# Sparse attention and a gated FFN on one core: the first K third through the casting queue, small tables over two issuers, and filler matmuls in column tiles

## The chip, the cores and the metric

The kernel runs on one core of a Trainium2 chip. Its engines are TensorE (PE, with its weight loads PEld), VectorE (DVE), ScalarE (ACT), GpSimd (POOL) and SyncE (SP). SP and ACT issue plain DMAs; POOL issues DMAs that change the type from float32 to float16 on the way. The metric is device microseconds (us) of one execution.

## The reference

```
q, k, v: 4 x 8 x 768 x 64 (batch, head, token, dim), float32
mask[i, j] over blocks of 32 tokens: |block i - block j| <= 1, or one of the two
    is the first or the last block, or j's block is one of 3 sampled for i's block
a = softmax(q k^T / 8 where mask else -1e9) v
x = a as 3072 tokens x 512
out = (sigmoid(x w_gate) * (x w_val)) w_out        # 512 -> 1536 -> 512
```

The output is 3072 x 512 in float32. The sampled blocks are an input, so the mask is made on the chip.

## The kernel before

The 3072 tokens are cut into twelve query chunks of 256 (three for each batch entry), and the eight heads into four pairs. For one chunk and pair (`attend`) there are three score tiles of two blocks of 128 keys each. A tile is made on PE by matmuls of 64 rows that stand in pairs in the two halves of the array, one for each head (L617); ACT takes the exponential (L635) and writes `pt`; DVE multiplies with the 0/1 mask (L643). When three tiles are done, 24 value matmuls follow (L658), DVE normalises (L666, L669), and the result is transposed into `xT`: on PE for the first three chunks (L694, copied by DVE at L699), by a DMA transpose later. In the first chunk the mask is not multiplied: extra matmuls (`e24` with `bias`, also L617) add a large negative number to masked scores, so that the exponential makes zeros of them.

The FFN (`ffn`) works on one query chunk of 256 tokens: for each of twelve blocks of 128 hidden units four gate and four value matmuls (L720), a tanh on ACT (L739), a product on DVE (L746); then twelve output matmuls for each of two blocks of 128 tokens (L764), scaled by 0.5 on ACT or DVE and stored by SP.

The order of the instructions on each engine is made by a planner (`Plan.run`), when the kernel is built. Each operation gets an engine, a duration, a priority and what it needs; the planner steps through a time of its own and gives each engine the best operation that is ready by that time. A load may name the time at which it is taken to have landed (`lands`, with the constants `LAND_K`, `LAND_Q`, `E24`). On the chip each engine then runs its list in order and waits where something is late. Where PE has nothing to do before the planned time `SPIN`, the planner puts in filler matmuls on a zero tile (`spin_op`, L364). From the `CHAIN`-th pair of chunk and head pair on, the order on PE is written out as fixed rounds (`ROUND`): score tiles, value matmuls, FFN and output matmuls. `FETCH` says behind which score tile the loads of the next batch entry may be issued; those of the second entry wait for the load of the second third of `wo` too.

The head of the kernel matters here. Of the first head pair of batch entry 0, K comes whole by SP into `k_in` (float32, L467) and a third of Q, the token positions that the first chunk needs (`early`, two of six), into `q_in` (L471). ACT casts the same third of K (`k_a`, L474) and of Q (`q_a`, L475), DVE casts the rest of K (`k_b`, L476). All the other loads of batch entry 0, in the order of `FIRST`, go by POOL with a cast (`load_half`, L423), and behind them the weights `wg`, `wv` (L503) and `wo` (L512), each in two or three parts. Q and K are then transposed on PE (`turn_pe`, L441) against the identity `ident16` and copied out of PSUM by ACT or DVE (L449, L447).

The small tables are `ident16`, `sbi` (the sampled blocks) and `mi` (fixed part of the mask and an index row), issued in this order by ACT (L342 to L344), and `e24` (which token is in which block), which SP loads twice, into rows 0 to 23 and 64 to 87 (L348). From `mi` and `sbi`, four small DVE operations (`blocks`, L540 to L546) make the mask of blocks, `mb16`. One matmul with `e24` (`expand`, L557) widens it, and DVE makes `bias` of it (L564). The array is used in three shapes: whole ("full"), in half rows ("row": scores and mask) and in half columns ("col": transposes of Q and K).

Of the kernel before, what the change touches and what calls it, by code (L numbers as in the profile page):

```python
# [9 lines left out]
f16 = mybir.dt.float16  # L10
f32 = mybir.dt.float32
# [6 lines left out]
NB = S // BLK  # L18
NJ = S // 128
# [8 lines left out]
VW = 66  # L28
SPIN = 22.0
NMASK = 1  # L30
FETCH = ((7, 1), (1, 2))
CHAIN, GLAG, OLAG, ROUND = 16, 5, 9, "SoVgggoo"
EDGES = [0, 768, 1536]
LAND_K, LAND_Q, E24 = 4.0, 4.7, 4.2
FIRST = [
    ("k", 1), ("q", 1), ("k", 2), ("q", 2), ("v", 0), ("q", 0), ("k", 3), ("q", 3), ("v", 1), ("v", 2), ("v", 3),
]
# [223 lines left out]
def kernel(  # L261
# [11 lines left out]
    nc = tc.nc  # L273
# [4 lines left out]
    e24_h = nc.inline_tensor(e24_np, name="bb_e24")  # L278
# [3 lines left out]
    mi_h = nc.inline_tensor(mi_np, name="bb_mdet_iota")  # L282
    id_h = nc.inline_tensor(np.eye(128, dtype=np.float16), name="bb_ident")
# [5 lines left out]
    src = {  # L289
        nm: [a[b].rearrange("h (p j) d -> p h j d", j=NJ) for b in range(B)]  # L290
        for nm, a in (("q", q), ("k", k), ("v", v))
    }
    outv = out.rearrange("(b p j) m -> b j p m", p=128, j=NJ)

    P = Plan()
# [11 lines left out]
    def sb(tag, shape, dt):  # L307
        n = len(P.rings[tag])
        return Buf(tag, lambda i: work.tile(shape, dt, tag=tag, bufs=n, name=tag))
# [4 lines left out]
    def psb(shape, dt=f32, homes=SINGLE, span=1):  # L314
        def make(i):
            t = psum[:, i : i + span].rearrange("p b c -> p (b c)")
            if dt != f32:
                t = t.bitcast(dt)
            n = int(np.prod(shape))
            t = t[:, 0:n]  # L320
            if len(shape) == 2:
                t = t.rearrange("p (a b) -> p a b", a=shape[0])
            return t

        b = Buf("ps", make)
        b.homes, b.span = homes, span
        return b

    def one(shape, dt, name):
        b = Buf(None, None)  # L330
        b.tile = sing.tile(shape, dt, name=name)
        return b


    ident16 = one([128, 128], f16, "ident16")
    sbi = one([NB, 3], mybir.dt.int64, "sbi")
    mi = one([NB, 2 * NB], f32, "mi")
    e24 = one([128, NJ, 128], f16, "e24")
    zero = one([128, 128], f16, "zero")
    P.op("DVE", 0.1, lambda: nc.vector.memset(zero(), 0.0), writes=[zero], prio=-91)  # L340
    P.op("DVE", 0.3, lambda: nc.vector.memset(e24(), 0.0), writes=[e24], prio=-99)
    P.op("ACT", 0.4, lambda: nc.scalar.dma_start(ident16(), id_h.ap()), writes=[ident16], prio=-99, dma=0.1, lands=3.0)  # L342
    P.op("ACT", 0.6, lambda: nc.scalar.dma_start(sbi(), sampled_blocks), writes=[sbi], prio=-98, dma=0.1, lands=3.4)  # L343
    P.op("ACT", 0.4, lambda: nc.scalar.dma_start(mi(), mi_h.ap()), writes=[mi], prio=-97, dma=0.1, lands=3.8)  # L344
    for i, r in enumerate((0, 64)):
        P.op(
            "SP", 0.45,
            lambda r=r: nc.sync.dma_start(e24()[r : r + NB].rearrange("b j q -> b (j q)"), e24_h.ap()),  # L348
            writes=[e24], prio=(-96, -93)[i], dma=0.2, lands=E24,
        ).deps[1:] = []  # L350
    vring = [one([128, 2, NJ, VW], f16, f"v16_{i}") for i in range(8)]
    for i in range(8):
# [3 lines left out]
            writes=[vring[i]], prio=-80 + i,  # L356
        )

    def spin_op(dur, fresh):
        if fresh:  # L360
            P.spun = psb([128])
        t = P.spun
        return P.op(
            "PE", dur, lambda: nc.tensor.matmul(t(), zero(), zero(), start=True, stop=True),  # L364
            reads=[zero], writes=[t], prio=1e6, mode="full",
        )

    P.spin, P.spin_op, P.spin_until = zero, spin_op, SPIN


    every, early, later = slice(0, NJ), slice(0, 2), slice(2, NJ)
# [42 lines left out]
    def load_half(nm, b, p, prio, dur=0.72):  # L414
        cut = (nm, b, p) == ("q", 0, 0)
        js = later if cut else every
        if cut:
            c = one([128, 2, NJ - 2, 64], f16, "q16_late")
        else:
            c = sb(f"{nm}16" if nm != "v" else "vh", [128, 2, NJ, 64], f16)  # L420
        half16[nm, b, p] = stage[nm, b, p] = c
        o = P.op(
            "POOL", dur, lambda: nc.gpsimd.dma_start(c(), src[nm][b][:, 2 * p : 2 * p + 2, js]),  # L423
            writes=[c], prio=prio, dma=0.8 if cut else 1.0,
        )
        o.slack = 0.3 + b
        return o
# [24 lines left out]
    def turn_dma(nm, b, p, prio):  # L452
# [6 lines left out]
            reads=[c], writes=[t], prio=prio, dma=1.3,  # L459
        )  # L460

    k_in = one([128, 2, NJ, 64], f32, "k_in")
    q_in = one([128, 2, 2, 64], f32, "q_in")
    k_a, k_b = one([128, 2, 2, 64], f16, "k16_a"), one([128, 2, NJ - 2, 64], f16, "k16_b")
    q_a = one([128, 2, 2, 64], f16, "q16_a")
    P.op(
        "SP", 0.5, lambda: nc.sync.dma_start(k_in(), src["k"][0][:, 0:2]), writes=[k_in], prio=-95, dma=1.0,  # L467
        lands=LAND_K,
    )
    P.op(  # L470
        "SP", 0.5, lambda: nc.sync.dma_start(q_in(), src["q"][0][:, 0:2, early]), writes=[q_in], prio=-94, dma=0.7,  # L471
        lands=LAND_Q,
    )
    P.op("ACT", 0.35, lambda: nc.scalar.copy(k_a(), k_in()[:, :, early]), reads=[k_in], writes=[k_a], prio=-88)  # L474
    P.op("ACT", 0.35, lambda: nc.scalar.copy(q_a(), q_in()), reads=[q_in], writes=[q_a], prio=-88)  # L475
    P.op("DVE", 0.42, lambda: nc.vector.tensor_copy(k_b(), k_in()[:, :, later]), reads=[k_in], writes=[k_b], prio=-67)  # L476
    for i, (nm, p) in enumerate(FIRST):
        last_in = load_half(nm, 0, p, -60 + i, 0.82 if i == 0 else 0.72)
    late = None
    for p in range(NP):  # L480
        if p == 0:
# [16 lines left out]
    n = 0  # L498
# [31 lines left out]


    eqs = one([NB, 3, NB], f32, "eqs")
    mb16 = one([NB, 128], f16, "mb16")
    bias = one([128, NJ, 128], f16, "bias")
    mask = one([128, NCH, NCH, 512], f16, "mask")
    P.op("DVE", 0.06, lambda: nc.vector.memset(mb16(), 0.0), writes=[mb16], prio=-90)
# [1 line left out]
    def blocks():  # L538
        d = nc.vector
        d.tensor_tensor(  # L540
            eqs()[:, 0:3], mi()[:, NB:].unsqueeze(1).to_broadcast([NB, 3, NB]),
            sbi().bitcast(u16)[:, 0:12:4].unsqueeze(2).to_broadcast([NB, 3, NB]), op=ALU.is_equal,
        )
        d.tensor_tensor(eqs()[:, 0], eqs()[:, 0], mi()[:, 0:NB], op=ALU.max)
        d.tensor_tensor(eqs()[:, 1], eqs()[:, 1], eqs()[:, 2], op=ALU.max)
        d.tensor_tensor(  # L546
            mb16().rearrange("p (a r) -> p a r", a=2)[:, :, 0:NB],
            eqs()[:, 0].unsqueeze(1).to_broadcast([NB, 2, NB]),
            eqs()[:, 1].unsqueeze(1).to_broadcast([NB, 2, NB]), op=ALU.max,
        )  # L550

    P.op("DVE", 0.5, blocks, reads=[sbi, mi], writes=[mb16, eqs], prio=-89)
    def expand(j0, n, prio, behind=()):
        pb = psb([n, 128])
        P.op(
            "PE", 0.1 * n,
            lambda pb=pb, j0=j0, n=n: nc.tensor.matmul(  # L557
                pb(), mb16(), e24()[0:NB, j0 : j0 + n], start=True, stop=True
            ),
            reads=[mb16, e24], writes=[pb], prio=prio, mode="full", behind=behind,  # L560
        )
        P.op(
            "DVE", 0.1 + 0.13 * n,
            lambda pb=pb, j0=j0, n=n: nc.vector.tensor_scalar(  # L564
                bias()[:, j0 : j0 + n], pb(), -1.0, BIG, op0=ALU.add, op1=ALU.mult
            ),
            reads=[pb], writes=[bias], prio=prio,
        )

    expand(0, 2, -89)  # L570
    mask_ops = {}

# [218 lines left out]
    for n in range(B * NCH):  # L791
        b, c = divmod(n, NCH)
# [10 lines left out]
        if b + 1 < B:  # L803
            for p in range(NP) if c == 0 else ():
# [5 lines left out]
                for nm in "kqv":  # L810
# [4 lines left out]
                    o.slack = 1.5  # L815
                    late_loads.append((12 * b + FETCH[b > 0][0] + FETCH[b > 0][1] * p, o))
                for nm in "kq":
# [59 lines left out]
```

The softmax here doesn't subtract the row's maximum and nothing guards it: scores larger than these inputs give would overflow.

## Time and profile before

| | us |
|---|---|
| median of 4 runs (lowest, highest) | 293.58 (292.49, 295.17) |
| the profiled execution, one of these four | 295.17 |
| its span, from the first to the last instruction | 293.4 |
| first score matmul / first exponential | 10.88 / 11.95 |
| first FFN matmul (L720) | 27.75 |
| PE busy, ACT busy, DVE busy | 286.2, 210.3, 193.4 |

The times in the profile count from the first instruction. A line of the timeline has the start, the length, the engine with the line of the kernel, the operation with its tiles and shapes, how many are drawn together, and in brackets how long the engine had been idle before and what ended that. A "q" behind the engine marks the issue of a DMA, which is not the transfer itself. A line of the chain has start, length, and what the chain was in. A landing time is counted from the start of the issue to the moment at which the data's semaphore is seen.

### The profile page before, as it was taken

How to read it: one execution, taken by the hardware profiler on the slowest of the kernel's cores; microseconds unless marked ns; L12 is line 12 of the kernel's file. 1: busy time of each engine (PE TensorE's matmuls, PEld its weight loads, DVE VectorE, ACT ScalarE, POOL GpSimd, SP SyncE). 2: the span in 40 equal slices, each digit the busy share in tenths (PEclk: the TensorE clock that was granted, in tenths of full speed). 3: DMA queues.
4: the chain of work that ended last, by engine and by line, in shares of the span. 5: the costliest groups of instructions: out<-in, count | busy, mean ns of one | idle time of the engine just before them, and what ended most of it. 6: DMA issues, size and time to landing. Idle time of an engine off the chain costs nothing.

```text
span 293.4 us, 8112 instructions
## 1 busy us (share of the span) xinstructions
PE 286.2 (98%) x3411; PEld 212.7 (72%) x3411; DVE 193.4 (66%) x451; ACT 210.3 (72%) x329; POOL 13.4 (5%) x22
## 2 busy tenths in 40 slices
PE   5999999999999999999999999999999999999995
PEld 4677786787677777777777777777776776777764
DVE  1448989887866876765876876765765765673330
ACT  2596779998988878768767777777777777773331
POOL 8630000000000000000000000000000000000000
PEclk9999999999999999999999999999999999999999
DMA  7999995995375965013566663110110120111003
GB/s 142 199 207 211 206 282 154 299 219 151 110 201 101 249 217 101 12 55 116 155 216 151 174 216 75 36 56 12 44 56 9 47 56 10 48 56 30 17 36 108
DMA packets 50516, 35.50 MB, mean 121 GB/s; under 512 B 31104, under 2 KB 47536, under 8 KB 50480
## 3 DMA queue, kind: packets, MB, share of 16 engines
q1 hardware_dynamic: 43576, 28.13, 34.6%
q0 software_dynamic: 6688, 6.82, 14.1%
q8 instruction: 26, 0.43, 0.6%
q14 instruction: 10, 0.08, 0.1%
q10 hardware_dynamic: 216, 0.04, 0.1%
HBM read 28.42 MB, written 6.29 MB: 118 GB/s over the span
## 4 chain that ended last, share of the span: by engine, by line
PE 91%; ACT 4%; DMA 2%; DVE 1%; issue 1%; ACTq 0%; DVEq 0%
PE psum L720 43%; PE psum L764 22%; PE psum L617 12%; PE psum L658 11%; ACT pt L635 3%; DMA mi<-bb_mdet_iota 2%; PE psum L441 1%; PE psum L579 1%; DVE pt L643 1%; PE psum L694 0%; PE psum L364 0%; ACT y L781 0%; PE psum L557 0%; ACTq L343 0%; DVE k L409 0%
## 5 line engine op out<-in xcount | busy, mean ns | idle before, releaser
L635 ACT ACTIVATE pt<-psum 128x1024 f16<-128x1024 f32 x144 | 139.0, 1031 | 21.7 <-PE psum L617 21.6
L643 DVE TENSOR_TENSOR pt<-pt,mask 128x1024 f16<-128x1024 f16 x132 | 89.7, 688 | 49.4 <-ACT pt L635 49.0
L720 PE MATMUL psum<-x,wv 128*128 128x256 f16 x576 | 86.5, 273 | 0.0
L720 PE MATMUL psum<-x,wg 128*128 128x256 f16 x576 | 86.4, 272 | 0.0
L739 ACT ACTIVATE tg<-psum 128x256 f32<-128x256 f32 x144 | 56.3, 393 | 38.9 <-PE psum L720 38.0
L764 PE MATMUL psum<-wo,h 128*128 128x512 f16 (+1 forms) x300 | 76.0, 372 | 0.1
L746 DVE SCALAR_TENSOR_TENSOR h<-tg,psum 128x256 f16<-128x256 f32 x144 | 58.3, 417 | 23.3 <-ACT tg L739 22.6
L720 PEld LDWEIGHTS <-wv 128*128 128x128 f16 x576 | 55.7, 98 | 7.6 <-issue 1.3
L720 PEld LDWEIGHTS <-wg 128*128 128x128 f16 x576 | 53.3, 98 | 8.3 <-issue 1.5
L658 PEld LDWEIGHTS <-pt 128*128 128x128 f16 x1152 | 42.6, 98 | 9.6 <-issue 0.6
L617 PE MATMUL psum<-qT,kT 64*128 64x256 f16 x576 | 45.5, 273 | 0.0
L658 PE MATMUL psum<-v,pt 128*128 128x65 f16 x1152 | 44.3, 193 | 0.0
L764 PEld LDWEIGHTS <-h 128*128 128x128 f16 x300 | 25.9, 98 | 22.4 <-issue 8.0
L617 PEld LDWEIGHTS <-kT 64*128 64x128 f16 x576 | 25.2, 95 | 19.1 <-issue 16.1
L781 ACT ACTIVATE y<-psum 128x512 f32<-128x512 f32 (+1 forms) x23 | 13.3, 579 | 12.7 <-PE psum L764 12.7
L669 DVE TENSOR_TENSOR x<-psum,rz 128x256 f16<-128x256 f32 x48 | 20.4, 425 | 1.9 <-DVE rz L666 0.3
L666 DVE RECIPROCAL rz<-psum 128x4 f32<-128x4 f32 x48 | 8.6, 180 | 5.2 <-PE psum L658 4.9
L364 PE MATMUL psum<-zero 128*128 128x128 f16 x43 | 5.3, 304 | 1.4 <-DVE zero L340 1.4
L617 PE MATMUL psum<-bias,e 64*128 64x256 f16 x48 | 6.4, 295 | 0.0
L587 DVE TENSOR_SCALAR mask<-psum 128x512 f16<-128x512 f32 x9 | 6.1, 683 | 0.1
L402 ACT CAST v<-vs 128x768 f16<-128x768 f32 x7 | 5.9, 842 | 0.0
L364 PEld LDWEIGHTS <-zero 128*128 128x128 f16 x43 | 4.3, 141 | 2.2 <-DVE zero L340 1.4
(55 smaller groups left out, 71.7 us busy)
## 6 DMA issues: line engine op xcount, KB each, us to landing
out_dram<-y SPq DMA_DIRECT2D x23, 256.0 KB, 2.6
ks<-in_k_dram SPq DMA_DIRECT2D x12, 384.0 KB, 3.8
qs<-in_q_dram SPq DMA_DIRECT2D x12, 384.0 KB, 4.2
vs<-in_v_dram SPq DMA_DIRECT2D x12, 384.0 KB, 5.1
wg<-in_moe_w_gate_dram POOLq DMA_DIRECT2D x2, 768.0 KB, 12.9
wv<-in_moe_w_val_dram POOLq DMA_DIRECT2D x2, 768.0 KB, 15.7
wo<-in_moe_w_out_dram POOLq DMA_DIRECT2D x3, 512.0 KB, 21.8
vh<-in_v_dram POOLq DMA_DIRECT2D x4, 192.0 KB, 7.4
```

The lines of the kernel that those rows point to most:

```text
L364: "PE", dur, lambda: nc.tensor.matmul(t(), zero(), zero(), start=True, stop=True),
L617: nc.tensor.matmul(st()[:, hd, jj * CH : (jj + 1) * CH], l[r, 2 * tt + jj, :], m[r, 2 * c : 2 * c + 2, :], start=not (own and masked), sto ...
L635: lambda st=st, pt=pt: nc.scalar.activation(pt().rearrange("p h j q -> p h (j q)"), st(), AF.Exp, scale=SCALE),
L643: nc.vector.tensor_tensor(t, t, mask()[:, c, tt].unsqueeze(1).to_broadcast([128, 2, 512]), op=ALU.mult)
L658: nc.tensor.matmul(o()[:, 2 * jq + hd, 0:65], pts[j // 2]()[:, hd, j % 2, jq * 128 : jq * 128 + 128], v_[:, hd, j, 0:65], start=(j == 0), ...
L666: P.op("DVE", 0.2, lambda: nc.vector.reciprocal(rz(), o()[:, :, 64:65]), reads=[o], writes=[rz], prio=seq - 5)
L669: lambda: nc.vector.tensor_tensor(x16().rearrange("p j (h d) -> p (j h) d", d=64), o()[:, :, 0:64], rz().to_broadcast([128, 4, 64]), op=AL ...
L720: nc.tensor.matmul(t()[:, z : z + w], wt()[:, i, f * 128 : (f + 1) * 128], xT[g, i]()[:, 0:w], start=(i == 0), stop=(i == NP - 1),)
L739: lambda tg=tg, a=pair[0]: nc.scalar.activation(tg()[:, 0:w], a[0]()[:, a[1] : a[1] + w], AF.Tanh, scale=0.5),
L746: lambda tg=tg, a=pair[1], h_=h_: nc.vector.scalar_tensor_tensor(h_()[:, 0:w], tg()[:, 0:w], 1.0, a[0]()[:, a[1] : a[1] + w], op0=ALU.add, ...
L764: nc.tensor.matmul(py()[:, m], hts[g, f]()[:, tt * 128 : (tt + 1) * 128], wo()[:, f, m], start=(f == 0), stop=(f == NF - 1),)
L781: lambda py=py, y=y, m=m: nc.scalar.activation(y()[:, m], py()[:, m], AF.Copy, scale=0.5),
```

## The change

- `mi` is issued by SP, as its first; ACT issues `sbi`, then `ident16`, then the second copy of `e24`. SP's second issue is the Q third, the third is the rest of K, the fourth the first copy of `e24`.
- The first K third is a POOL load with cast into `k_a`, ahead of all other POOL loads; its cast on ACT goes away. `k_in` holds only the rest (four of six), and ACT casts it instead of DVE. The copies out of PSUM of the first K and Q thirds stand on DVE in the new order instead of ACT.
- DVE clears the spin tile before `e24`.
- Filler matmuls use 64 columns of the array ("col") instead of 128; the planner places 47 of them instead of 43.
- `expand` becomes two matmuls of 64 columns over all 128 rows, so it needs both copies of `e24`, and `mb16` has 128 rows.
- The planner's landing times are given one for each load; `CHAIN` goes from 16 to 18 and the first `FETCH` from 7 to 6.

```diff
-FETCH = ((7, 1), (1, 2))
-CHAIN, GLAG, OLAG, ROUND = 16, 5, 9, "SoVgggoo"
+FETCH = ((6, 1), (1, 2))
+CHAIN, GLAG, OLAG, ROUND = 18, 5, 9, "SoVgggoo"
-LAND_K, LAND_Q, E24 = 4.0, 4.7, 4.2
+LAND = dict(sbi=2.9, mi=2.4, ident=3.1, e0=3.6, e1=3.9, q=2.9, kb=3.8, k=3.6)
...
-    P.op("DVE", 0.3, lambda: nc.vector.memset(e24(), 0.0), writes=[e24], prio=-99)
-    P.op("ACT", 0.4, lambda: nc.scalar.dma_start(ident16(), id_h.ap()), writes=[ident16], prio=-99, dma=0.1, lands=3.0)
-    P.op("ACT", 0.6, lambda: nc.scalar.dma_start(sbi(), sampled_blocks), writes=[sbi], prio=-98, dma=0.1, lands=3.4)
-    P.op("ACT", 0.4, lambda: nc.scalar.dma_start(mi(), mi_h.ap()), writes=[mi], prio=-97, dma=0.1, lands=3.8)
-    for i, r in enumerate((0, 64)):
+    P.op("DVE", 0.38, lambda: nc.vector.memset(e24(), 0.0), writes=[e24], prio=-90)
+    P.op(
+        "ACT", 0.65, lambda: nc.scalar.dma_start(sbi(), sampled_blocks), writes=[sbi], prio=-99, dma=0.1,
+        lands=LAND["sbi"],
+    )
+    P.op(
+        "ACT", 0.4, lambda: nc.scalar.dma_start(ident16(), id_h.ap()), writes=[ident16], prio=-98, dma=0.1,
+        lands=LAND["ident"],
+    )
+    P.op("SP", 0.3, lambda: nc.sync.dma_start(mi(), mi_h.ap()), writes=[mi], prio=-99, dma=0.1, lands=LAND["mi"])
+    for i, (eng, q, r) in enumerate((("SP", nc.sync, 0), ("ACT", nc.scalar, 64))):
...
-            "PE", dur, lambda: nc.tensor.matmul(t(), zero(), zero(), start=True, stop=True),
-            reads=[zero], writes=[t], prio=1e6, mode="full",
+            "PE", dur, lambda: nc.tensor.matmul(t()[0:64], zero()[:, 0:64], zero(), start=True, stop=True),
+            reads=[zero], writes=[t], prio=1e6, mode="col",
...
+    k_in, q_in = one([128, 2, NJ - 2, 64], f32, "k_in"), one([128, 2, 2, 64], f32, "q_in")
     P.op(
-        "SP", 0.5, lambda: nc.sync.dma_start(k_in(), src["k"][0][:, 0:2]), writes=[k_in], prio=-95, dma=1.0,
-        lands=LAND_K,
+        "SP", 0.5, lambda: nc.sync.dma_start(q_in(), src["q"][0][:, 0:2, early]), writes=[q_in], prio=-95, dma=0.7,
+        lands=LAND["q"],
     )
     P.op(
-        "SP", 0.5, lambda: nc.sync.dma_start(q_in(), src["q"][0][:, 0:2, early]), writes=[q_in], prio=-94, dma=0.7,
-        lands=LAND_Q,
+        "SP", 0.5, lambda: nc.sync.dma_start(k_in(), src["k"][0][:, 0:2, later]), writes=[k_in], prio=-94, dma=1.0,
+        lands=LAND["kb"],
     )
-    P.op("ACT", 0.35, lambda: nc.scalar.copy(k_a(), k_in()[:, :, early]), reads=[k_in], writes=[k_a], prio=-88)
+    P.op(
+        "POOL", 0.82, lambda: nc.gpsimd.dma_start(k_a(), src["k"][0][:, 0:2, early]), writes=[k_a], prio=-95,
+        dma=0.5, lands=LAND["k"],
+    )
     P.op("ACT", 0.35, lambda: nc.scalar.copy(q_a(), q_in()), reads=[q_in], writes=[q_a], prio=-88)
-    P.op("DVE", 0.42, lambda: nc.vector.tensor_copy(k_b(), k_in()[:, :, later]), reads=[k_in], writes=[k_b], prio=-67)
+    P.op("ACT", 0.56, lambda: nc.scalar.copy(k_b(), k_in()), reads=[k_in], writes=[k_b], prio=-67)
...
-    mb16 = one([NB, 128], f16, "mb16")
+    mb16 = one([128, 128], f16, "mb16")
...
-            "PE", 0.1 * n,
-            lambda pb=pb, j0=j0, n=n: nc.tensor.matmul(
-                pb(), mb16(), e24()[0:NB, j0 : j0 + n], start=True, stop=True
-            ),
-            reads=[mb16, e24], writes=[pb], prio=prio, mode="full", behind=behind,
+            lambda pb=pb, j0=j0, n=n: [
+                nc.tensor.matmul(
+                    pb()[r : r + 64], mb16()[:, r : r + 64], e24()[:, j0 : j0 + n], start=True, stop=True
+                )
+                for r in (0, 64)
+            ],
+            reads=[mb16, e24], writes=[pb], prio=prio, mode="col", behind=behind,
```

## The prediction

> **What bounds the kernel now.** I read the page's busy shares first, then the timeline of the first 30 us, the waits of that stretch, the landings of the weights, and last the chain in one round of the steady part.
>
> ```profile
> PE 286.2 (98%) x3411; PEld 212.7 (72%) x3411; DVE 193.4 (66%) x451; ACT 210.3 (72%) x329; POOL 13.4 (5%) x22
> PE   5999999999999999999999999999999999999995
> ```
>
> TensorE looks full from the second slice on, but "busy" counts filler and half-clock work too. From the chain, one round of the steady part (24 FFN matmuls, 4 output matmuls, 12 scores, 2 outputs, 24 values):
>
> ```profile
> 100.51 2.62 PE psum L720 x24
> 103.13 0.86 PE psum L764 x4
> 103.99 0.76 PE psum L617 x12
> 104.75 0.54 PE psum L764 x2
> 105.29 0.76 PE psum L658 x24
> ```
>
> The next round begins at 106.05, so a round is 5.54 us. Per instruction that is 0.109 us for an FFN matmul (2.62/24), 0.215 for an output matmul (0.86/4), 0.0545 for a score matmul (a pair side by side in 0.109), 0.032 for a value matmul. These make 2.62 + 1.29 + 0.65 + 0.77 = 5.33; the missing 0.21 lies at the two changes of array shape (into and out of the half-row scores): 0.1 us each. Counted over the instruction order of before, all that follows the first FFN matmul is 253.7 us of such work with 100 changes of shape. The first FFN matmul starts at 27.75, the last matmul ends at 290.35: 262.6 us, so 253.7 + 100 x 0.09. After 27.75 TensorE has no hole; the end moves only with the start of the FFN, and with what is added to the order behind it. What sets 27.75 is the head:
>
> ```profile
> 1.91 0.30 ACTq L344 DMA_DIRECT2D mi<-bb_mdet_iota  x1
> 1.40 3.92 PE L364 MATMUL psum<-zero 128*128 128x128 f16 x35 [1.40 <-DVE zero L340]
> 6.97 0.22 DVE L540 TENSOR_TENSOR eqs<-mi,sbi 24x72 f32<-24x72 f32 x1 [5.31 <-DMA mi<-bb_mdet_iota]
> 8.14 0.41 ACT L475 CAST q_a<-q_in 128x256 f16<-128x256 f32 x1 [3.27 <-DMA q_in<-in_q_dram]
> 8.20 0.72 POOL L423 DMA_DIRECT2D vh<-in_v_dram  x1 [1.16 <-DMA k<-in_k_dram]
> 11.95 1.94 ACT L635 ACTIVATE pt<-psum 128x1024 f16<-128x1024 f32 x2 [2.02 <-PE psum L617]
> 12.35 0.42 PE L617 MATMUL psum<-qT,kT 64*128 64x256 f16 x2
> 13.53 0.27 PE L617 MATMUL psum<-qT,kT 64*128 64x256 f16 x2
> 15.43 8.46 ACT L635 ACTIVATE pt<-psum 128x1024 f16<-128x1024 f32 x9 [0.34 <-PE psum L617]
> 27.75 0.61 PE L720 MATMUL psum<-x,wg 128*128 128x256 f16 x4
> ```
>
> To be seen: the mask table `mi` lands 5 us after its issue and the Q third at 8.1 us, so the first scores stand at 10.88, the first exponential at 11.95, and the twelve exponentials of the first query chunk end at 23.89. From there to the FFN (two pairs' values, normalisation, transposes, copies) it is 3.86 us. The FFN also needs its weights:
>
> ```profile
> DMA to landing us min/median/max: 12.8/15.7/18.6
> ```
>
> These are the two loads of `wv`, issued at 12.28 and 13.95: they land at 25.1 and 32.6. The last `wo` (issued 16.96, 23.2 to landing) is there at 40.2.
>
> **The change part by part.**
>
> *Tables and first loads.* `mi` becomes SP's first issue (0.73) instead of ACT's third (1.91), `sbi` ACT's first. The row for a first small load is `ident`: issued 0.73, 2.7 us to landing. So both are there near 3.5, the mask blocks (6.97 to 7.73 before, 0.76 us) near 4.4. `q_in` moves from SP's third place behind 384 KB of K to its second (issue near 1.1) with nothing large ahead. Best row: `k_in`, first on that queue, 384 KB in 3.7 us; a third of it about 3 us: landing near 4.0, cast done near 4.5 (0.41, L475). ACT's table load (2.24 to 3.52) is pushed by three ACT issues of 0.70 + 0.41 + 0.43 to about 3.7, still under the wait. K's rest (256 KB, SP) lands near 5, and its cast goes from DVE to ACT, idle there. Both `e24` halves are now needed by the expansion; SP's half queues behind K's rest, about 5.3.
>
> *The K third on POOL.* One more cast load ahead of all others. The trace has none of this size. One end: the Trainium skill, "DMA: Bandwidth & Descriptors", section "Anatomy of one DMA — SWDGE (gpsimd) path", gives 2.0 us plus bytes/436 GB/s; 64 KB written behind an issue that ends at 2.05 would land at 4.2. The other end: the first POOL load of before (192 KB) releases the waiting POOL issue only at 8.20, although issued at 1.24. The same page ("Latency and other measured facts") speaks against the move too: first byte 1 us on this path, 0.6 us on SP's. By the rule first scores come near 7, by the row near 10. I take 5, first scores near 7.2. It matters little: the order puts the transposes of pair 1's K ahead of pair 0's third score tile, and of pair 2's K ahead of pair 1's scores. Those loads landed at about 8.2, 9.3, 10.3, 11.3 (POOL releases at 8.20, 9.35, 10.33, 11.31: one load per us). With the extra third ahead of them and 128 KB less on SP's queue I add 0.3. Pair 2's K is then there at 10.6, 12 transposes at half clock 0.85 (row 9.31), two score tiles 0.86 and two changes of shape: pair 1's first exponential at about 12.6 against 15.43, whether the third lands at 4.2 or 8.2. In the second case pair 0's three exponentials end at 13.1: 0.5 us is its whole price.
>
> *Exponentials.* Nine remain at 8.46/9 = 0.94: they end at 21.1, against 23.89. Plus 3.86: FFN possible at 25.0. But `wv` lands at 25.1 + 0.3. FFN start 25.4: 2.35 us earlier. From here the weights would be late next: the second half of the weight columns is wanted 8 us after the start (33.6, there at 32.9), the first output matmul 15.1 us after (40.5, `wo` at 40.2 + 0.3). Both just hold; so more than 2.4 us is not to be had.
>
> *Order behind it.* `CHAIN` 18 and `FETCH` 6 change the hand-over to the fixed rounds. In the two orders after the first FFN matmul the same FFN, output and value matmuls stand; scores go from 516 to 520 (+0.22), changes of shape from 100 to 108 (+0.8). Cost 1.0 us. The loads of batch 1 still wait for the second `wo` (SP's first issue stands at 37.67, where that `wo` lands), so their chain of casts and transposes does not move; batch 1's first scores come 65 us in by both orders. Below it could cost 0.2 (all eight drains under some wait), above 2 (a DVE or ACT instruction placed too early holds its queue; those engines have 34% and 28% slack).
>
> *Spins and expansion in column tiles.* 47 spins for 43 and 4 expansion matmuls for 2, all ahead of the FFN; the shape changes they save there are under the waits: 0. What counts is the clock. The Trainium skill, "TensorE: Matmul & The Clock Gate", Part 1, opens the clock after about 3.4 us of sustained activity in a free-running window; Part 4 says that transposes don't count as busy in the same way. In the trace 35 full-array spins of 112 ns over 3.9 us did not open it; score matmuls take 0.42 us at 12.35 and 0.27 at 13.53, so it opened near 13. By the rule, with filler from 1.2 us on, it would open by 8; by the row not before 13; half-array filler with holes could miss one window more (16.7). Work from 12.6 to the FFN is some 9 us warm plus 2 us of changes of shape, in 12.8 us: 2 us spare. One window more costs 2.2 us of TensorE time, nearly covered; two windows (20.1) cost 3.9 and put the FFN near 27.4. I take the row: 0, ends 0 and +2.
>
> **Sum.** -2.35 + 1.0 = -1.3 us. Against the profiled execution (295.17, span 293.38 and 1.8 around it) this gives 293.9; that run is the slowest of the four shown, 1.6 above their median. Against the median, 293.58: 292.3.
>
> **Rivals.**
> - *The weights hide it.* POOL's loads slip by a whole place (1 us) behind the K third: `wv` at 26.1, FFN at 26.2: -1.5 + 1.0 = -0.5, 293.1. For: the cadence of one load per us; against: the bytes only move between queues.
> - *It doesn't bring Q earlier.* If the Q third straggles as before (8.1), exponentials start at 11, pair 1 follows at 14 to 15.4, the FFN starts near 27: -0.7 + 1.0 = +0.3, 293.9. Against: its packets would be out before POOL's flood begins (POOL's queue moves its first packets past 3 us).
> - *The clock stays low (slower).* Half-array spins and transposes leave it shut until 20: FFN at 27.4 or later, -0.3 + 1.0 to +2, 294.3 to 295.5. It decides from an FFN start past 26.7.
> - *More gain.* SP's queue empties before POOL's flood, POOL's loads run 1 us earlier, and the changes of shape cost nothing: FFN 24.6, -3.1 + 0.2 = -2.9, 290.7.
>
> **How the numbers follow.** Forecast 0.45, weights 0.2, Q late 0.12, clock or a stall behind the hand-over 0.15, more gain 0.08. A measurement of this kernel can tell about 1% (2.9 us) from no change. The forecast's own range is 291.2 to 293.4; to hold 8 in 10 it reaches to 290.5 below and 295.0 above. Faster by over 1% needs the last case or better: 0.12. Slower by over 1% needs the clock's worst or a stall beyond 2 us: 0.13. Within: 0.75.
>
> **What would show it.** Right: mask blocks done before 5, first exponential near 8 with a hole of 1 to 2 us ahead of pair 1's, twelfth ending near 21, first FFN matmul at 25 to 26, and 264 us from there to the last matmul. Wrong: L720 starting after 26.7; score matmuls of 0.42 us past 17; a first output matmul waiting for `wo`; or over 265 us behind the FFN's start.

## The result, and the profile after

The changed kernel takes 293.49 us in the median of 43 runs (292.53 to 294.85); the kernel before takes 293.92 in the median of 64 (291.73 to 295.55). The ratio is 0.9987, with a 95% interval of 0.9976 to 0.9999: 0.4 us gained, where 1.3 were forecast. The profiled execution took 293.94 us, with a span of 292.0. Against the profile of before (295.17 and 293.4) that is 1.2 to 1.4 us, just what was forecast. So the two profiles agree with the forecast and the medians don't. Why is the question of this study.

One thing no profile shows: in 11 of the changed kernel's runs the time exceeds the span by 2.4 to 3.0 us, in the others by 1.7 to 2.2, in the 147 runs of before beside the experiments by 1.7 to 1.9. What it is stays open. It hardly moves the median (the median span, 291.7, and 1.8 make 293.5 too).

PE is busy 98% of the span as before (285.5 us against 286.2). The timeline, the lines that answer to those of before (L370 is the filler, L483 and L484 the casts of Q and of the K rest, L566 the expansion, L628 the scores, L646 the exponentials, L731 the FFN):

```profile
0.99 3.01 PE L370 MATMUL psum<-zero 128*64 128x128 f16 x27 [0.99 <-DVE zero L340]
2.53 0.22 DVE L548 TENSOR_TENSOR eqs<-mi,sbi 24x72 f32<-24x72 f32 x1 [0.86 <-DMA sbi<-in_sampled_blocks_dram]
3.93 0.40 ACT L483 CAST q_a<-q_in 128x256 f16<-128x256 f32 x1 [0.37 <-DMA q_in<-in_q_dram]
6.38 0.62 ACT L484 CAST k_b<-k_in 128x512 f16<-128x512 f32 x1 [2.05 <-DMA k_in<-in_k_dram]
6.96 0.30 PE L566 MATMUL psum<-e,mb 128*64 128x256 f16 x2 [2.05 <-DMA e<-bb_e]
8.43 0.42 PE L628 MATMUL psum<-qT,kT 64*128 64x256 f16 x2
9.32 1.02 ACT L646 ACTIVATE pt<-psum 128x1024 f16<-128x1024 f32 x1 [2.31 <-PE psum L628]
11.07 0.27 PE L628 MATMUL psum<-qT,kT 64*128 64x256 f16 x2
12.98 2.85 ACT L646 ACTIVATE pt<-psum 128x1024 f16<-128x1024 f32 x3 [0.35 <-PE psum L628]
19.71 2.86 ACT L646 ACTIVATE pt<-psum 128x1024 f16<-128x1024 f32 x3 [0.19 <-PE psum L628]
25.70 0.61 PE L731 MATMUL psum<-x,wg 128*128 128x256 f16 x4
```

Tables and Q third are there early, but now the K rest and `e24` are late, and PE idles for 2 us ahead of the expansion. This idle stretch between the first fillers and the expansion is called the hole below, and all that stands ahead of the first FFN matmul the head. The first exponential moves from 11.95 to 9.32, the twelfth ends at 22.57 instead of 23.89, the FFN starts at 25.70 instead of 27.75. The end of the chain:

```profile
280.28 2.62 PE psum L731 x24
282.90 6.09 PE psum L775 x40
```

The last matmul ends at 288.99: 263.3 us behind the FFN's start, against 262.6 before.

What was overlooked stands in the stretches of this profile (columns: stretch, length, PE busy and instructions, granted clock, DMA share, GB/s):

```profile
4.00:6.00 2.00, 0.52 (x10) 1.00 1.08 191
6.00:8.00 2.00, 1.04 (x17) 0.80 1.23 173
8.00:10.00 2.00, 2.00 (x18) 0.50 1.26 181
10.00:12.00 2.00, 2.00 (x38) 0.85 1.32 192
```

The trace's clock record has the clock opened at 3.79 us, by the filler alone, shut at 7.20 and opened again at 10.61, in steps of 3.41 us. PE stood idle from 4.91 to 6.96 (the row of the expansion has 2.05), and the scores from 8.24 on ran at half clock (0.42 against 0.27). In the profile of before the clock opened once, at 13.27. (Before the first entry of that record the column shows 1.00 whatever the clock is; there only the matmuls' lengths tell it.)

### The profile page after: what moved, and what is told of

It is laid out like the page before. It is cut to its first block, busy times and chain, and to the rows that moved or that the text cites. A ratio compares the mean times of both kernels' runs of the same rounds, so it can differ in the third digit from the quotient of the medians.

```text
span 292.0 us, 8127 instructions
## 1 busy us (share of the span) xinstructions
PE 285.5 (98%) x3417; PEld 211.4 (72%) x3417; DVE 196.0 (67%) x458; ACT 206.7 (71%) x321; POOL 14.1 (5%) x23
## 3 DMA queue, kind: packets, MB, share of 16 engines
q0 software_dynamic: 6960, 6.88, 14.4%
## 4 chain that ended last, share of the span: by engine, by line
PE 97%; DMA 2%; ACT 0%; issue 0%
PE psum L731 44%; PE psum L775 23%; PE psum L628 14%; PE psum L669 13%; DMA e<-bb_e 2%; PE psum L447 1%; PE psum L590 1%; PE psum L705 1%; DMA sbi<-in_sampled_blocks_dram 1%; PE psum L370 0%; PE psum L566 0%; ACT y L792 0%
## 5 line engine op out<-in xcount | busy, mean ns | idle before, releaser
L646 ACT ACTIVATE pt<-psum 128x1024 f16<-128x1024 f32 x144 | 139.1, 1026 | 24.1 <-PE psum L628 24.0
L731 PE MATMUL psum<-x,wv 128*128 128x256 f16 x576 | 86.5, 273 | 0.0
L731 PE MATMUL psum<-x,wg 128*128 128x256 f16 x576 | 86.4, 272 | 0.0
L731 PEld LDWEIGHTS <-wv 128*128 128x128 f16 x576 | 55.5, 98 | 7.9 <-issue 1.7
L731 PEld LDWEIGHTS <-wg 128*128 128x128 f16 x576 | 53.5, 98 | 7.8 <-issue 1.3
L628 PE MATMUL psum<-qT,kT 64*128 64x256 f16 x576 | 45.4, 273 | 0.0
L628 PEld LDWEIGHTS <-kT 64*128 64x128 f16 x576 | 24.6, 95 | 19.6 <-issue 16.7
L792 ACT ACTIVATE y<-psum 128x512 f32<-128x512 f32 (+1 forms) x22 | 12.7, 577 | 12.3 <-PE psum L775 12.3
L370 PE MATMUL psum<-zero 128*64 128x128 f16 x47 | 5.7, 283 | 1.0 <-DVE zero L340 1.0
L628 PE MATMUL psum<-bias,e 64*128 64x256 f16 x48 | 6.5, 294 | 0.0
L370 PEld LDWEIGHTS <-zero 128*64 128x64 f16 x47 | 4.6, 152 | 1.6 <-DVE zero L340 1.0
L415 DVE CAST k<-ks 128x768 f16<-128x768 f32 x10 | 5.5, 553 | 0.0
```

The lines of the kernel that those rows point to most:

```text
L370: "PE", dur, lambda: nc.tensor.matmul(t()[0:64], zero()[:, 0:64], zero(), start=True, stop=True),
L628: nc.tensor.matmul(st()[:, hd, jj * CH : (jj + 1) * CH], l[r, 2 * tt + jj, :], m[r, 2 * c : 2 * c + 2, :], start=not (own and masked), sto ...
L646: lambda st=st, pt=pt: nc.scalar.activation(pt().rearrange("p h j q -> p h (j q)"), st(), AF.Exp, scale=SCALE),
L731: nc.tensor.matmul(t()[:, z : z + w], wt()[:, i, f * 128 : (f + 1) * 128], xT[g, i]()[:, 0:w], start=(i == 0), stop=(i == NP - 1),)
L792: lambda py=py, y=y, m=m: nc.scalar.activation(y()[:, m], py()[:, m], AF.Copy, scale=0.5),
```

## The experiments

Each was compared with runs of before on the same chip, so the ratios can be compared with one another. FFN start and the time behind it (from the first FFN matmul to the end of the last matmul) are from each run's one profile:

| run | ratio to before (95%) | clock opens for good | FFN start | behind it |
|---|---|---|---|---|
| before / changed kernel | 1 / 0.9987 | 13.27 / 10.61 | 27.75 / 25.70 | 262.6 / 263.3 |
| x1 before again | 0.9987 (0.9969 to 1.0005) | 10.82 | 26.11 | 262.6 |
| x2 changed, CHAIN 16 | 1.0074 (1.0054 to 1.0095) | 12.65 | 26.68 | 265.5 |
| x3 before, CHAIN 18 | 1.0006 (0.9992 to 1.0020) | 13.82 | 27.65 | 262.6 |
| x4 changed, e24 first | 1.0067 (1.0049 to 1.0085) | 11.85 | 26.34 | 263.3 |
| x5 before, tables and Q | 0.9973 (0.9957 to 0.9990) | 13.42 | 27.18 | 262.6 |
| x6 changed, POOL held | 1.0071 (1.0044 to 1.0098) | 15.71 | 27.45 | 263.4 |
| x7 changed, K third on SP | 1.0093 (1.0061 to 1.0125) | 11.41 | 26.80 | 263.3 |
| x8 changed, e24 on ACT | 0.9994 (0.9975 to 1.0014) | 12.68 | 26.67 | 263.3 |
| x9 changed, filler | 0.9968 (0.9955 to 0.9980) | 5.76 | 24.32 | 264.0 |
| x10 as x5, filler | 0.9929 (0.9904 to 0.9953) | 5.12 | 24.35 | 262.6 |
| x11 changed, full-array filler | 1.0005 (0.9981 to 1.0029) | 4.51 | 24.20 | 263.7 |
| x12 before, no filler | 0.9980 (0.9964 to 0.9996) | 11.82 | 25.77 | 262.5 |
| x13 before, filler | 0.9949 (0.9932 to 0.9965) | 5.66 | 25.00 | 262.6 |
| x14 as x10, no filler later on | 0.9928 (0.9898 to 0.9957) | 5.90 | 23.99 | 262.6 |
| x15 as x10 | 0.9936 (0.9915 to 0.9957) | 5.73 | 24.30 | 262.6 |

**x1: before, unchanged.**

> The kernel before, unchanged, looked at once more. Theory A (the profile that the forecast was built on was a late draw: its Q third and its mask table landed later than they usually do): in this second profile the first FFN matmul stands near 26.5 instead of 27.75, the span is near 292.2 instead of 293.4, and the work behind it again takes 262.6 us. Theory B (the head is the same each time, and the change's gain is lost behind the FFN's start): the first FFN matmul is again within 0.3 of 27.75. Time ratio 1.000 under both.

Its timeline:

```profile
6.00 0.22 DVE L540 TENSOR_TENSOR eqs<-mi,sbi 24x72 f32<-24x72 f32 x1 [4.34 <-DMA mi<-bb_mdet_iota]
7.17 0.41 ACT L475 CAST q_a<-q_in 128x256 f16<-128x256 f32 x1 [2.21 <-DMA q_in<-in_q_dram]
10.98 11.26 ACT L635 ACTIVATE pt<-psum 128x1024 f16<-128x1024 f32 x12 [2.02 <-PE psum L617]
26.11 0.61 PE L720 MATMUL psum<-x,wg 128*128 128x256 f16 x4
```

Theory A holds: this execution's FFN starts 1.6 us earlier than in the profile of before, the span is 1.6 shorter, and what follows takes 262.6 us to the tenth. The tables landed 1 us earlier, and the clock opened 2.45 us earlier, so that no exponential had to wait for PE. The head of before varies; the rest does not. Five profiles have before's own loads (before, x1, x3, x12, x13). The one that the forecast was built on is the latest of them: its table ended the wait at 6.97, in the others at 6.00 to 6.37, and its Q cast stands at 8.14, in the others at 7.17 to 7.44.

**x2 and x3: the hand-over.** x2 is the changed kernel with the old constants, x3 the kernel before with the new ones:

```diff
-FETCH = ((6, 1), (1, 2))
-CHAIN, GLAG, OLAG, ROUND = 18, 5, 9, "SoVgggoo"
+FETCH = ((7, 1), (1, 2))
+CHAIN, GLAG, OLAG, ROUND = 16, 5, 9, "SoVgggoo"
```

> The changed kernel with CHAIN back at 16 and FETCH back at 7: 102 changes of array shape behind the FFN's start instead of 108, the same work. If a change of shape costs 0.1 us wherever it stands: 0.6 us faster than the changed kernel, 292.9, ratio to before 0.9965. Theory B (the hand-over eats the gain): over 1 us faster than the changed kernel, ratio below 0.995. Rival, the hand-over costs nothing: ratio 0.9985 as the changed kernel.

> The kernel before with CHAIN 18 and FETCH 6 alone: its order has the same 100 changes of shape and the same work behind the FFN's start. If only counts matter: ratio 1.000 within 0.001. Theory B (the later hand-over itself stalls PE): ratio 1.003 or more.

x3 moved nothing. x2 missed on every side: with fewer changes of shape it is 0.9% slower than the changed kernel. Its chain shows what the count can't:

```profile
73.05 0.34 PE psum L628 x4
73.39 0.02 issue
73.42 1.03 ACT pt L646
...
85.06 0.38 ACT tg L750
85.44 4.23 ACT pt L646 x5
```

Twice the chain leaves PE for ACT: PE stands for exponentials that the order asks for too early, and 265.5 us go by behind the FFN's start instead of 263.3. The new constants are needed by the new head; they are not its cost. The 0.7 us between 263.3 and 262.6 stay. The order has eight changes of shape and four scores more there, which would account for them; no run separates the two.

**x4 and x8: e24.** x4 gives `e24`'s first copy on SP a priority ahead of the K rest; x8 has both copies on ACT:

```diff
-            writes=[e24], prio=-93, dma=0.2, lands=LAND[f"e{i}"],
+            writes=[e24], prio=(-94.5, -93)[i], dma=0.2, lands=LAND[f"e{i}"],
```

```diff
-    for i, (eng, q, r) in enumerate((("SP", nc.sync, 0), ("ACT", nc.scalar, 64))):
+    for i, (eng, q, r) in enumerate((("ACT", nc.scalar, 0), ("ACT", nc.scalar, 64))):
```

> The changed kernel with SP's copy of e24 issued ahead of the K rest instead of behind it. In the changed kernel's profile e24 landed at 6.93 and held the expansion, the bias and so the first scores (8.24). If e24 lands near 5, the expansion moves to where the K rest decides, first exponential near 8.3 instead of 9.32. Theory A with the weights as the next bound: pair 1's exponentials wait for its loads, the FFN's start stays at 25.7 within 0.3 and the time does not move (ratio 0.9985). Rival, the head still decides: FFN 0.7 earlier, ratio 0.996.

> The changed kernel with both copies of e24 issued by ACT, none by SP. ACT's queue has only small tables ahead of them. If the place behind the K rest made e24 late (6.93): it lands before 5.5 and the K rest is not hurt (6.4), so that first scores move from 8.24 to about 7.8, first exponential 8.9, FFN near 25.4, ratio 0.997. If every packet that is out after POOL's flood begins is late, whatever its queue: e24 past 6, nothing moves, ratio 0.9985.

In x4 the expansion ran at 4.82, but the cast of the K rest slid from 6.38 to 7.25, and the first scores came no earlier: the wait was handed on. The six runs lose 0.8% against the changed kernel. The profiled one is the fastest of them (294.43, median 295.80), so where the rest of the loss lies stays open. In x8 the K rest was cast at 5.09, and `e24` still held the expansion to 6.88. In both, the load that stands last comes past 6 us.

**x6: POOL held.** Pair 1's K, and all POOL loads behind it, wait for the K rest:

```diff
+            if (nm, b, p) == ("k", 0, 1):
+                tc.add_manual_dep(
+                    ins.ins, landed["kin"].ins.name,
+                    mybir.DependencyInfo(mybir.DependencyClass.Sync, mybir.DependencyReason.DATA),
+                    reason="after the K rest",
+                )
```

> The changed kernel, orders unchanged, with POOL's load of pair 1's K (and so all POOL loads behind it) held until the K rest on SP has landed. If POOL's cast loads starve the plain queues: K rest and e24 land near 4.8 instead of 6.38 and 6.93, first exponential near 8; the price is a later wv (over 26 instead of 25.2), FFN near 26.5 and ratio 1.002. If the plain queues are slow by themselves: K rest and e24 stay past 6, and only the loss remains, ratio 1.005.

```profile
5.22 0.62 ACT L493 CAST k_b<-k_in 128x512 f16<-128x512 f32 x1 [0.88 <-DMA k_in<-in_k_dram]
5.52 0.30 PE L575 MATMUL psum<-e,mb 128*64 128x256 f16 x2 [0.28 <-DMA e<-bb_e]
7.05 1.94 ACT L655 ACTIVATE pt<-psum 128x1024 f16<-128x1024 f32 x2 [1.22 <-PE psum L637]
27.45 0.61 PE L740 MATMUL psum<-x,wg 128*128 128x256 f16 x4
```

Without POOL's flood the K rest is cast 1.16 us earlier, the expansion runs 1.4 earlier and the first exponential 2.3. One profile on each side can't carry these sizes: with the same loads and POOL not held, the K rest was cast at 6.38, 5.91, 6.46 and 5.42 (changed kernel, x2, x9, x11), and the expansion ran at 6.96, 6.93 and 6.32 (changed kernel, x2, x11). For `e24` x6 is 0.8 earlier than the earliest of these, for the K rest only 0.2. So POOL's cast loads hold up `e24`, as far as one profile can show it; for the K rest it isn't shown. As they feed pair 1 and the weights, holding them costs more than it gives: PE waited 1.36 and 1.49 us for K of the next pairs, the clock shut from 12.30 to 15.71, and the FFN started at 27.45.

**x7: the K third on SP**, in float32 behind the Q third, cast by ACT. The planner placed 40 fillers instead of 47; behind the FFN's start the counts are the same.

```diff
-        "POOL", 0.82, lambda: nc.gpsimd.dma_start(k_a(), src["k"][0][:, 0:2, early]), writes=[k_a], prio=-95,
+        "SP", 0.5, lambda: nc.sync.dma_start(k_e(), src["k"][0][:, 0:2, early]), writes=[k_e], prio=-94.5, dma=0.7,
...
+    P.op("ACT", 0.35, lambda: nc.scalar.copy(k_a(), k_e()), reads=[k_e], writes=[k_a], prio=-87)
```

> The changed kernel with the first K third taken from POOL: SP issues it in float32 between the Q third and the K rest, ACT casts it. If the K third's place on the cast queue brings the gain: it lands later on SP, the first scores slip by 0.5 or more, ratio 1.000. My forecast held its landing worth 0.5 us at most: POOL's loads move up by one place (pair 1's K by 0.3), the K rest slips by 0.5, FFN within 0.4 of 25.7, ratio 0.998 to 1.000.

```profile
7.78 0.62 ACT L486 CAST k_b<-k_in 128x512 f16<-128x512 f32 x1 [1.76 <-DMA k_in<-in_k_dram]
8.10 0.43 PE L568 MATMUL psum<-e,mb 128*64 128x256 f16 x2 [1.72 <-DMA e<-bb_e]
```

This is the largest miss: 1% slower than the changed kernel. The third's own landing matters little: its cast stands at 5.62, ahead of the K rest. What it pushes back on SP's queue matters: K rest and `e24` come 1.4 and 1.1 us later than in the changed kernel, and later than in any profile with that kernel's loads. That isn't all of the loss. There are seven fillers fewer, the mean clock of three of the six runs is 0.986 to 0.988 (a longer shut time than in any run of the changed kernel), and the profile is again the fastest run (295.32, median 296.68).

**x5: only tables and Q.** The kernel before with its orders on PE, DVE and POOL untouched:

```diff
-    P.op("ACT", 0.4, lambda: nc.scalar.dma_start(mi(), mi_h.ap()), writes=[mi], prio=-97, dma=0.1, lands=3.8)
+    P.op("SP", 0.4, lambda: nc.sync.dma_start(mi(), mi_h.ap()), writes=[mi], prio=-100, dma=0.1, lands=3.8)
...
```

with `sbi` ahead of `ident16` on ACT, and `q_in` ahead of `k_in` on SP, by their priorities.

> The kernel before with its orders on PE, DVE and POOL unchanged: mi is SP's first issue and sbi ACT's first, and SP issues the Q third ahead of K. Nothing else. If the early tables and Q alone bring the gain: first exponential about 2 us earlier than in the second look at before (10.98), near 9, ratio 0.994 or less. Theory (what counts is the new order on PE: in the old one the transposes of pair 1's K and Q stand ahead of pair 0's scores, and pair 1's Q lands near 8.9): tables near 2.5, Q near 4, and yet the first exponential near 10.6, ratio 0.998 to 1.000.

The median is 293.16, a little better than theory allowed, and its interval overlaps that of the changed kernel. So the better part of the change can be had by reordering four issues. Its profile was one of the late executions (294.59): PE waited from 5.32 to 6.73, and the clock opened at 13.42.

```profile
10.88 1.94 ACT L635 ACTIVATE pt<-psum 128x1024 f16<-128x1024 f32 x2 [2.02 <-PE psum L617]
27.18 0.61 PE L720 MATMUL psum<-x,wg 128*128 128x256 f16 x4
```

This is the other half of x1. The order on PE is the same, and the first exponential stands at 10.88 against x1's 10.98; but the clock opened 2.6 us later than in x1, and the FFN started 1.07 later.

**x9, x10, x13: filler in the hole.** Ahead of the first expansion PE gets 28, 20 or 24 more fillers, which write the bank that the expansion overwrites; x9 in the changed kernel, x10 in x5's, x13 in the kernel before. As in x13:

```diff
-            lambda pb=pb, j0=j0, n=n: nc.tensor.matmul(
+            lambda pb=pb, j0=j0, n=n: [
+                nc.tensor.matmul(
+                    pb().rearrange("p a b -> p (a b)")[:, 0:128], zero(), zero(), start=True, stop=True
+                )
+                for _ in range(24 if j0 == 0 else 0)
+            ] + [nc.tensor.matmul(
```

> The changed kernel with 28 more filler matmuls on PE just ahead of the first expansion, where PE stood idle for 2.2 us (4.73 to 6.96) in its profile; all other orders are the same. In that profile the clock opened at 3.8, shut at 7.2 and opened again at 10.6. Theory C (the clock's window runs free, the hole shuts the clock, and which window it falls into makes the spread of the times): the clock no longer shuts near 7, the scores from 8.2 on take 0.27 instead of 0.42, the FFN starts near 25.2, the spread shrinks from 2.3 us to 1.5 and the ratio is 0.995 to 0.997. Rival (the weights' landing at 25.2 binds, the clock does not): FFN not ahead of 25.3, ratio 0.9985. Where the clock is still shut, 28 fillers take 3.0 us and push the expansion 0.8 back.

> The kernel before with the tables' and the Q third's issues moved as in the fifth run (ratio 0.9973) and 20 more filler matmuls ahead of the first expansion, where PE waited 1.4 us for e24. Theory C: the clock stays open more often, ratio 0.995. Rival as in the ninth run: ratio 0.997.

> The kernel before with 24 more filler matmuls ahead of the first expansion, nothing else; there PE stood idle for 2.5 us in its profile (1.5 in the second look). Theory C (the hole shuts the clock): the clock opens by 6 in most executions and stays open, FFN near 25.2 although the mask table still lands near 6 and Q near 7, ratio 0.995 to 0.996. Rival (the landings are what counts): ratio 0.998 to 1.000, since expansion and Q cast are as late as before.

x13's timeline:

```profile
6.28 0.22 DVE L540 TENSOR_TENSOR eqs<-mi,sbi 24x72 f32<-24x72 f32 x1 [4.62 <-DMA mi<-bb_mdet_iota]
7.44 0.40 ACT L475 CAST q_a<-q_in 128x256 f16<-128x256 f32 x1 [2.51 <-DMA q_in<-in_q_dram]
5.11 1.77 PE L558 MATMUL psum<-zero 128*128 128x128 f16 x24
7.08 0.28 PE L562 MATMUL psum<-e,mb 24*128 24x256 f16 x1 [0.21 <-DVE mb L546]
9.12 0.27 PE L622 MATMUL psum<-qT,kT 64*128 64x256 f16 x2
25.00 0.61 PE L725 MATMUL psum<-x,wg 128*128 128x256 f16 x4
```

Table and Q are as late as in x1 (by 0.3 us later), but PE is never idle for long, the clock opens at 5.66 and stays open, and the scores take 0.27 from the first. That alone gives 0.9949, more than the whole change, and the runs lie within 292.08 to 292.77. With early tables and Q (x10 and its repetition x15) it is 0.9929 and 0.9936. In the changed kernel (x9) the next bound shows: a wait for the weights inside the FFN's first block.

```profile
24.32 0.61 PE L736 MATMUL psum<-x,wg 128*128 128x256 f16 x4
25.49 0.61 PE L736 MATMUL psum<-x,wv 128*128 128x256 f16 x4 [0.56 <-DMA wv<-in_moe_w_val_dram]
```

**x11: full-array filler in the changed kernel.**

```diff
-            "PE", dur, lambda: nc.tensor.matmul(t()[0:64], zero()[:, 0:64], zero(), start=True, stop=True),
+            "PE", dur, lambda: nc.tensor.matmul(t(), zero(), zero(), start=True, stop=True),
```

> The changed kernel with filler matmuls over 128 columns instead of 64, orders unchanged. If half-array filler counts for the clock as the full one does: ratio 0.9985 as the changed kernel, within 0.001. If full-array filler opens the clock more often: ratio 0.996 and an open clock before 6 in the profile. If the change of shape between filler and transposes costs something: 4 changes more ahead of the scores, 0.4 us, ratio 1.000.

Inconclusive on the time: the interval holds the changed kernel's ratio and each of the theories but the best one. Its profiled execution took 292.93, the third lowest of its 14; others took up to 295.63. In that profile the clock opened at 4.51 and stayed open over a hole of 1.26 us (5.06 to 6.32).

**x12: no filler at all** in the kernel before (the planned fillers emit nothing).

> The kernel before without any filler matmul, all other orders the same. Theory C: nothing can open the clock before real work has filled a window, so it opens once, between 10 and 15, in every execution; the times gather where before has its later group (294.6 to 295.5): ratio 1.002 to 1.004. Rival (filler is worth nothing in before, since its wait of 2.5 us shuts the clock again): ratio 1.000 within 0.001.

Theory C missed here: 0.9980, better than before. As expected the clock opens once, by real work (11.82). What was not reckoned with is that fillers between transposes and scores cost time on the path: from the expansion to the first scores it is 2.16 us here (6.94 to 9.10) against 3.1 in before (7.78 to 10.88).

**x14: as x10, with fillers only ahead of the first expansion.**

> The tenth run's kernel without the 8 filler matmuls between the transposes and scores; those ahead of the first expansion stay. They cost about 0.5 us between expansion and first score at the open clock (0.94 at half clock, from the twelfth run against the second look). If the weights bind: first exponential 0.4 earlier, FFN no earlier than the landing of wv near 24.4, ratio 0.9925 to 0.993. If the exponentials still decide: FFN 0.4 earlier, ratio 0.9915.

The FFN starts at 23.99 in its profile, 0.36 before x10, and its first `wv` matmul at 24.45, just behind the landing of `wv` (issued 10.53, 13.9 to landing). The times don't tell x14 from x10 (0.9928 and 0.9929).

**x15: x10 again.**

> The tenth run's kernel once more, unchanged. It gave 0.9929 (0.9904 to 0.9953) from six runs: the same within 0.0015, so 0.9915 to 0.9945.

It did.

## Why the prediction failed

**The frame held.** In sixteen of the seventeen profiles the time behind the FFN's start hardly moves: 262.5 to 262.6 by before's order and 263.3 to 263.7 by the changed kernel's (264.0 with x9's wait), where the forecast had 262.6 and 263.6. Only x2, with a hand-over that fits no head, left it. The order's cost was 0.7, not 1.0.

**The steps of the head.** Forecast and seen in the profile: mask blocks done 4.4 and 3.3; Q cast done 4.5 and 4.3; K third 5 and 4.3; K rest 5 and 6.4; `e24` 5.3 and 6.9; first scores 7.2 and 8.24; pair 1's exponential 12.6 and 12.98; the twelfth ending 21.1 and 22.57; FFN 25.4 and 25.70. The K rest and `e24` were sized by loads that had the queue to themselves; with POOL held (x6) they come at 5.2 and 5.5, near the forecast. For the K third the estimate from the Trainium skill's fixed cost ("DMA: Bandwidth & Descriptors", "Anatomy of one DMA — SWDGE (gpsimd) path") gave 4.2 and my row 8.2; 4.3 was measured. That this landing is worth 0.5 us at most was not contradicted; what the text left out is that on SP the third would push back the K rest and `e24` by more than 1 us (x7).

That the FFN came out so near is in part luck. The twelfth exponential ended 1.5 us later than forecast. From there to the FFN I took before's 3.86 us; in the changed kernel it is 3.13. The same 3.83 to 3.87 stands in all eight other profiles by before's order, and 3.13 or 3.14 in all others by the changed kernel's but x7 (3.41). So the new order gives ahead of the FFN's start the 0.7 us that it costs behind it, and what the change truly moves in its profile is the twelfth exponential: 1.3 us, not 2.8.

**The step that failed** is the last line of the sum: "Against the median, 293.58: 292.3". The 2.35 us were taken from an execution whose FFN started at 27.75, and subtracted from a median whose FFN starts earlier. The text said that this execution lay 1.6 us above the median, and did not ask where these 1.6 us were. x1 shows them in the head. The starts that belong to the medians can be estimated by working back (1.8 around the span, 3.0 from the last matmul to the end of the span): the FFN of before starts near 293.92 - 1.8 - 3.0 - 262.6 = 26.5, that of the changed kernel near 293.49 - 1.8 - 3.0 - 263.3 = 25.4. So by this estimate the FFN's forecast start (25.4) was right, and the gain of the head is 1.1 us, not 2.35; less 0.7 for the order, that is the 0.4 measured.

**Why the head varies** was wrong too: it is the term for the clock, which the sum put at 0. I read from one row (35 fillers, clock still at half) that filler doesn't open the clock. By the Trainium skill, "TensorE: Matmul & The Clock Gate", Part 1, the window of about 3.4 us runs free of the kernel. The records agree: 3.79, 7.20 and 10.61 are 3.41 apart, and between executions the first opening shifts. The filler of before fills 3.9 us (1.40 to 5.32); how much of one window it covers is luck. Counted back in steps of 3.41 from the first opening (an estimate, as the record has no earlier entry), PE was busy for 82% of the window that opened the clock at 3.79 in the changed kernel. The fullest window of filler in x1 (0.58 to 3.99) had 76%, that of before (3.03 to 6.45) 67%, and the clock stayed shut.

The runs show what this makes of the times. The mean granted clock counts from the first opening on, so it tells whether the clock was shut again (one shut window of 3.4 us in 292 makes 0.994), but not how late it opened. Of the 147 runs of before beside the experiments, 83 have 0.994 or less, with a median span of 292.0. These are not the slow ones. Among the other 64, which by their mean clock opened once, 26 have spans of 290.0 to 291.8, and 38 have 292.4 to 293.8, like the profile of before (293.4, opened once, at 13.27). Of the changed kernel's 44 executions on record (the 43 and one more) 12 were shut again, and their median span is 292.0 as well; of the others only three lie above 292.4. So among executions that shut again the change gains nothing, and what it gains is that fewer are late.

How much a late clock costs can be read from the table. In four profiles of the changed kernel's head the first scores stand at 8.24 to 8.43; the FFN starts at 25.70 where the clock opened for good at 10.61, at 26.34 for 11.85 (x4), at 26.68 and 26.67 for 12.65 and 12.68 (x2, x8). By x5 against x1 a clock 2.6 us later is 1.07. So of x1's 1.6 us about 1.1 are the clock's and the rest the landings' (an estimate from that pair). The rival "the clock stays low" had the right mechanism, but I took it for a risk of the change, when it lay in both kernels. Its cure (x13) was worth more than the change: with table and Q as late as ever and only the hole filled, the range of the runs shrinks from 3.3 us (before, beside x13) to 0.7, and none of the 15 shows a shut window.

**The version to keep** is x10's: early tables and Q, filler in the hole, the old order behind. It beats before by 0.6 to 0.7% in two runs of it; the changed kernel reaches 0.1%.

## What to carry to other kernels

A profile is one draw: before a gain in a stage is taken from it, ask how far the execution lies from the median and in which stage the difference sits, and take a second profile of the same kernel. Where filler work is to keep TensorE's clock open, it has to run up to the first real work; here 20 to 28 matmuls in the hole gave 0.2 to 0.5% (x9, x10, x13), and without them the kernel's own 43 were worth nothing (x12). When a load is taken from a queue, ask first what stands behind it there: in x7 that weighed more than the load's own landing.

## What the runs showed of the hardware

Matmuls on zeros opened the clock of TensorE, of 64 columns (at 3.79 us in the changed kernel's profile, with the first filler at 0.99) as of 128 (at 4.51 in x11). It opened and shut in steps of 3.41 us (3.79, 7.20, 10.61; in x4 5.03, 8.44, 11.85). Once open, it shut at the end of a window in which PE had been busy for 0.97 of the 3.41 us (changed kernel, 3.79 to 7.20) or for 1.72 (x6, 8.88 to 12.30). It stayed open over one with 2.15 (x11, 4.51 to 7.92) and one with 2.20 (x6, 5.47 to 8.88). With 28 half-array fillers in the hole it stayed open (x9).

For opening, the busy share alone doesn't decide. Besides the 82% that opened it and the 76% of filler that didn't, windows counted back in the same way were 94% and 96% busy, mostly with the transposes of Q and K (x3 up to 10.41, x5 up to 10.01), and left it shut. Why stays open.

With POOL's cast loads held back, `e24` let the expansion run at 5.52 (x6), without that at 6.32 to 6.96 (changed kernel, x2, x11); the K rest was cast at 5.22 against 5.42 to 6.46.
